# A new step order, one residual on TensorE and two more transposes by DMA in a two-block transformer kernel

## The chip, the cores and the metric

The kernel runs on one core of one Trainium2 chip. A core has five engines that run beside each other and meet through semaphores: TensorE (PE in the profile, with PEld for its weight loads), VectorE (DVE), ScalarE (ACT), GpSimd (POOL) and SyncE (SP, which here issues DMAs). The metric is the device time of one launch in microseconds (us). Before, three runs took 214.1, 212.67 and 212.69 us; their median is 212.69.

## The reference

The input x has 2048 rows of 512 elements in bf16. Two blocks follow each other, each with a layer norm ahead and a residual around it:

```
h  = x + A(layernorm(x))
h2 = h + B(layernorm(h))

A: qkv = x @ wqkv (512 x 1536), 32 heads of 16
   each position attends to 8 positions: itself and those 2, 4, ... 14 before it
   logits = q . k * 16**-0.5, those before the start masked; softmax over the 8; sum of v; @ wo (512 x 512)
B: gate = x @ W_gate, up = x @ W_up (512 x 1376)
   h = relu(gate) * up;  h @ W_down (1376 x 512)
layernorm: (x - mean) / sqrt(var + 1e-5), with no weights
```

## The kernel before

**Tiles.** The 2048 rows are four chunks (0 to 3, `tk` in the code) of 512 rows, each of four blocks of 128 rows. The whole of x stays in one tile `x_sm`, which the first residual overwrites in place with h. All weights are resident. Working tiles come from small pools that are shared by purpose: 9 `quad` tiles (a transposed norm, q, or the attention output: 128 x 4 x 512), 5 `big` tiles (128 x 8 x 512, the products of the attention), 5 `row` tiles (one normalised block of 128 x 512, or one output block), and 8 PSUM banks named `bank`, which every matmul group takes and an eviction frees.

**Stages of one chunk**, with the names that the steps carry below:

- first norm of x: statistics on VectorE (L420, L423), a logarithm and an exponential on ACT (L433, L437), the normalised blocks `xxn` on VectorE (L455, into `row`), and their transposes into a `quad` tile
- q, k and v: 12 groups of four 128x512 matmuls (L525, 4 x 0.216 us = 0.864 us), each evicted by ACT (L533)
- scores: products `pr` of q with eight shifted views of k on VectorE (L572, 2.2 us each, four a chunk), summed within heads on PE (L578), an exponential on ACT (L594), the denominators `den` on PE (L611), a logarithm and an exponential for their reciprocal on ACT (L614, L617). Chunk 0 scales with that reciprocal at the end (steps `om`, L667); chunks 1 to 3 scale the weights early (`am`, L626)
- weights spread back to channels on PE (L639, steps `bc`), evicted by ACT (L645); products `mu` with v on VectorE (L660, 2.2 us each, four a chunk); their sum over eight positions as a tree. In chunks 0 to 2 the first level of the tree is an accumulating DMA that GpSimd issues (L692, steps `ta`, 512 KB each); the rest is VectorE (L663, L686)
- `wo` on PE (L712, four groups of four matmuls, one group a block) and the first residual (L723): VectorE adds x and writes h into `x_sm`, with the row sums for the second norm
- second norm of h: mean and squares (L401 on VectorE, L409 on ACT with a sum), L430 and L437 on ACT, `hxn` on VectorE (L455), and transposes into a `quad` tile, hnT
- up and gate: 22 groups (L750, steps `mmu` and `mmg` by slice 0 to 10 of the 1376 columns), evicted by ACT (L754, and L757 with the relu), multiplied on VectorE (L770, steps `gu`, two slices at a time, each from a pair of tiles of which there are two)
- down: four blocks, each in two pieces of 8 and 3 matmuls (L787, steps `dn` a and b), the second residual on VectorE (L798, steps `o`), and the store by SP (L802, steps `os`). The last block of chunk 3 is cut in two halves of 256 columns.

**Two ways to transpose.** A normalised block is transposed either by four identity matmuls on PE (L484), with ACT evicting two blocks at once (L500; VectorE for two blocks of chunk 0, L498), or by a transposing DMA that SP issues from the `row` tile straight into the `quad` tile (L473). The tuple `DMAT` lists the pairs of blocks that go by DMA, each as (norm, chunk, first block): x of chunk 3 and h of chunks 2 and 3.

**Order.** The code first lists all steps (`add`), each with its engine and what it depends on. `RANK` holds one number per step, in the order of listing. Each engine runs its steps in the order of that number, so every queue (PE, VectorE, ACT, SP, GpSimd) is fixed by hand, and a step whose operands are late holds all that is behind it on its engine. `Plan.order` walks through the queues with assumed durations to choose which buffer of a pool each step takes. The chunks overlap widely: the products q, k, v of chunks 1 to 3 run on PE while VectorE works on chunk 0's attention, and the MLP of one chunk runs beside the attention of later ones.

**Around the change.** On VectorE, before: `xxn` of chunk 2, then mu3, mu0 of chunk 0, two `xxn` of chunk 3, mu1, mu2, and the other two `xxn` of chunk 3. SP issues each transpose as its block is ready. GpSimd issues `ta` as each `mu` is ready. The settings read by the changed code are `DMAT` (L468) and `RPE` (L406 to L411, L712 to L729), the chunks whose first residual goes to PE; before it is empty.

Of the kernel before, what the change touches and what calls it, by code (L numbers as in the profile page):

```python
# [15 lines left out]


RANK = [
    0, 1, 2, 3, 4, 5, 6, 7, 8, 9, 10, 11, 12, 13, 14, 15, 16, 18, 19, 21,
    25, 27, 28, 17, 20, 22, 24, 26, 31, 34, 38, 30, 35, 37, 39, 41, 44, 47, 23, 29,  # L20
    32, 33, 36, 40, 43, 50, 62, 71, 46, 64, 69, 42, 53, 65, 48, 52, 55, 56, 74, 67,
    77, 76, 82, 72, 79, 88, 90, 95, 148, 89, 97, 84, 99, 101, 94, 112, 118, 122, 78, 86,
    93, 96, 100, 157, 169, 192, 127, 134, 133, 138, 141, 102, 115, 110, 121, 105, 158, 167, 202, 206,
    211, 170, 182, 226, 231, 234, 180, 188, 229, 233, 236, 146, 159, 199, 204, 208, 244, 249, 241, 246,
    247, 253, 238, 243, 256, 262, 252, 254, 257, 260, 248, 250, 265, 269, 274, 277, 276, 280, 283, 278,
    282, 281, 285, 289, 313, 317, 321, 343, 335, 339, 345, 353, 358, 326, 337, 292, 300, 298, 336, 315,
    327, 347, 330, 351, 346, 355, 338, 359, 348, 356, 364, 319, 325, 296, 302, 309, 314, 301, 305, 331,
    357, 365, 341, 362, 352, 374, 366, 376, 383, 354, 371, 361, 368, 382, 417, 433, 459, 545, 380, 430,
    456, 460, 372, 389, 424, 461, 405, 414, 454, 463, 49, 59, 45, 57, 54, 60, 51, 58, 61, 63,
    73, 80, 68, 83, 85, 66, 81, 70, 87, 91, 163, 172, 152, 181, 104, 107, 142, 153, 106, 113,  # L30
    136, 176, 130, 145, 161, 174, 116, 155, 120, 164, 165, 178, 98, 103, 212, 193, 235, 239, 237, 219,
    251, 258, 263, 267, 273, 286, 284, 304, 312, 307, 311, 308, 290, 295, 293, 297, 299, 318, 324, 367,
    370, 334, 344, 375, 379, 342, 349, 386, 388, 322, 333, 373, 377, 395, 399, 400, 408, 392, 397, 398,
    403, 401, 404, 410, 413, 402, 406, 407, 409, 415, 416, 419, 423, 420, 425, 427, 422, 428, 421, 426,
    431, 438, 453, 445, 449, 437, 440, 443, 446, 464, 488, 502, 491, 496, 483, 500, 480, 490, 520, 470,
    477, 457, 469, 448, 455, 434, 458, 479, 465, 472, 475, 492, 452, 467, 478, 485, 494, 522, 537, 513,
    534, 462, 482, 517, 538, 546, 526, 540, 524, 528, 542, 543, 552, 556, 668, 530, 555, 566, 569, 539,
    553, 582, 586, 549, 557, 568, 587, 111, 124, 92, 108, 117, 123, 75, 109, 129, 131, 137, 156, 135,
    147, 160, 140, 150, 144, 149, 162, 186, 203, 184, 189, 201, 207, 179, 228, 194, 200, 183, 185, 205,
    217, 224, 230, 195, 198, 175, 223, 197, 209, 171, 220, 266, 259, 287, 291, 294, 288, 306, 316, 328,  # L40
    332, 340, 363, 360, 369, 378, 385, 381, 384, 387, 396, 393, 394, 391, 441, 450, 486, 489, 435, 444,
    481, 484, 429, 436, 466, 468, 412, 439, 471, 474, 498, 505, 495, 499, 509, 515, 501, 508, 514, 518,
    504, 506, 519, 521, 512, 523, 525, 527, 532, 550, 533, 536, 529, 541, 544, 547, 602, 607, 620, 626,
    597, 617, 593, 609, 630, 577, 581, 563, 583, 574, 592, 571, 576, 604, 588, 590, 594, 599, 584, 601,
    580, 605, 613, 567, 572, 565, 573, 561, 564, 559, 562, 579, 627, 641, 623, 632, 634, 639, 631, 645,
    649, 606, 616, 589, 648, 651, 646, 656, 658, 667, 652, 657, 683, 726, 636, 660, 663, 666, 655, 659,
    661, 664, 114, 126, 128, 143, 132, 139, 119, 125, 151, 154, 166, 177, 190, 196, 168, 173, 187, 191,
    227, 242, 210, 214, 264, 275, 215, 245, 218, 222, 255, 272, 261, 270, 221, 225, 232, 240, 213, 216,
    268, 329, 271, 279, 303, 310, 320, 323, 390, 350, 411, 418, 432, 442, 447, 503, 451, 507, 516, 531,
    511, 510, 473, 487, 497, 493, 476, 535, 558, 575, 595, 560, 570, 578, 598, 585, 591, 596, 603, 548,  # L50
    551, 554, 600, 608, 611, 610, 614, 612, 625, 615, 622, 619, 624, 618, 621, 628, 629, 633, 635, 637,
    638, 644, 654, 640, 643, 642, 653, 647, 650, 679, 692, 670, 688, 662, 695, 684, 687, 697, 691, 703,
    672, 675, 694, 699, 682, 685, 706, 689, 693, 698, 702, 686, 690, 677, 700, 705, 669, 676, 674, 678,
    671, 673, 665, 680, 681, 710, 715, 696, 712, 701, 717, 707, 709, 719, 708, 711, 704, 714, 716, 720,
    727, 729, 737, 723, 728, 731, 734, 713, 722, 724, 725, 718, 721, 733, 735, 730, 732, 736, 738,
]


# [129 lines left out]
def kernel(  # L188
# [147 lines left out]
    DAL = 5.5  # L336
    TDD, TDL = 1.25, 1.5
    NWARM, NFILL = 44, 8
    DMAT = (('h',2,0),('h',2,2),('x',3,0),('x',3,2),('h',3,0),('h',3,2))

    EARLY = (1, 2, 3)

    RPE, OPE = (), ()

    MERGE = (0, 1, 2, 3)

# [39 lines left out]
    def layernorm(tk, src, dst_slots, pr, groups, on_act, residual=None):  # L386
# [7 lines left out]
        for grp in groups:  # L394
# [72 lines left out]
            for j0 in range(lo, hi, step):  # L467
                if (ln, tk, j0) in DMAT:  # L468
                    for j in range(j0, min(j0 + step, hi)):
# [385 lines left out]
```

## Time and profile before

| | |
|---|---|
| three runs | 214.1, 212.67, 212.69 us (median 212.69) |
| the profiled execution: its time | 214.1 us |
| its span, first to last instruction | 212.3 us |
| mean granted TensorE clock | 0.984 |
| PE busy | 196.1 us |
| VectorE, ACT, GpSimd busy | 155.4, 121.9, 12.9 us |
| up and gate, 352 matmuls (L750) | 84.4 us |
| q, k, v, full-width groups of four (L525) | 0.864 us each at the full clock |
| transposes by DMA (L473) | 12 |
| accumulating DMAs (L692) | 12, median 6.0 us to landing |
| first residual (L723) | 16 x 0.684 us on VectorE |

The profile shows one execution. A row of a timeline has the start and the length in us, the engine, the line, the operation, the tiles (out<-in), shapes, and in brackets the idle time before it with what ended it. A busy PE is not proof of a PE at its peak, since matmuls are pipelined; the granted clock tells how fast it ran. The chain that ended last goes back from the last instruction, at each step to what released it. Busy times are sums over the whole span, and the limits differ from stage to stage.

### The profile page before, as it was taken

The numbers are of one execution on the slowest core, as the hardware profiler recorded it, in microseconds if no ns is written. First come the engines' busy times: TensorE is split into PE (matmuls) and PEld (weight loads), VectorE is DVE, ScalarE is ACT, GpSimd is POOL, SyncE is SP. The second block draws the span as 40 slices with busy tenths as digits, with TensorE's granted clock in tenths as the row PEclk, the third lists the DMA queues.
The fourth block names the chain that finished last, engine by engine and source line by source line (L and its number), as shares of the span: only waits on it lengthen the run. The fifth ranks groups of instructions, "written<-read, shape, count | busy, mean of one in ns | idle before, by whom it ended". The sixth has DMA issues, their size and how long they took to land.

```text
span 212.3 us, 2963 instructions
## 1 busy us (share of the span) xinstructions
PE 196.1 (92%) x1119; PEld 95.9 (45%) x1119; DVE 155.4 (73%) x247; ACT 121.9 (57%) x249; POOL 12.9 (6%) x29
## 2 busy tenths in 40 slices
PE   7699899980699999999999999999999999999993
PEld 7475345530243444444445444444444444444542
DVE  6678999997534999999999977599995642022213
ACT  3467699750176998659773759950445850167500
POOL 3000002300000000230002400000000000000000
PEclk9999999998599999999999999999999999999999
DMA  5689951998200000397000992032010022200012
GB/s 180 215 246 398 394 162 38 181 167 65 43 3 0 0 0 3 67 191 137 3 0 0 198 204 74 0 74 49 28 49 0 0 56 46 99 0 0 0 48 79
DMA packets 16589, 18.57 MB, mean 87 GB/s; under 512 B 7264, under 2 KB 13376, under 8 KB 16576
## 3 DMA queue, kind: packets, MB, share of 16 engines
q0 software_dynamic: 1728, 6.29, 18.2%
q1 hardware_dynamic: 14272, 11.31, 17.6%
q10 hardware_dynamic: 576, 0.79, 1.2%
q8 instruction: 9, 0.15, 0.3%
q14 instruction: 4, 0.03, 0.0%
HBM read 8.42 MB, written 2.10 MB: 50 GB/s over the span
## 4 chain that ended last, share of the span: by engine, by line
PE 61%; DVE 23%; DMA 12%; issue 2%; ACT 0%; POOL 0%; DVEq 0%; ACTq 0%; POOLq 0%
PE bank L750 27%; PE bank L787 18%; DVE big L572 10%; DVE big L660 7%; DMA x_sm<-in_A_x_dram 7%; PE bank L712 7%; PE bank L525 6%; DMA quad<-row 5%; DVE st L420 2%; DVE row L455 1%; PE bank L578 1%; DVE gT L770 1%; DVE ex L626 1%; PE bank L484 0%; PE bank L639 0%
## 5 line engine op out<-in xcount | busy, mean ns | idle before, releaser
L750 PE MATMUL bank<-quad,wg_sb 128*128 128x512 bf16 (+1 forms) x176 | 42.2, 379 | 0.1
L750 PE MATMUL bank<-quad,wu_sb 128*128 128x512 bf16 (+1 forms) x176 | 42.2, 379 | 0.0
L754 ACT CAST up_sb<-bank 128x512 bf16<-128x512 f32 (+1 forms) x44 | 24.8, 595 | 26.4 <-PE bank L750 18.8
L525 PE MATMUL bank<-quad,wqk_sb 128*128 128x512 bf16 (+1 forms) x144 | 30.9, 364 | 9.5 <-DMA quad<-row 8.3
L787 PE MATMUL bank<-wd_sb,gT 128*128 128x512 bf16 (+3 forms) x187 | 39.6, 367 | 0.1
L572 DVE TENSOR_TENSOR big<-quad,kT 128x4096 bf16<-128x4096 bf16 x16 | 36.0, 2282 | 1.0 <-ACT kT L533 1.0
L660 DVE TENSOR_TENSOR big<-big,vT 128x4096 bf16<-128x4096 bf16 x16 | 36.0, 2283 | 0.1
L757 ACT ACTIVATE gr<-bank 128x512 bf16<-128x512 f32 (+1 forms) x44 | 25.6, 607 | 15.4 <-PE bank L750 14.8
L770 DVE TENSOR_TENSOR gT<-gr,up_sb 128x1024 bf16<-128x1024 bf16 (+1 forms) x24 | 15.1, 640 | 18.4 <-ACT gr L757 12.4
L787 PEld LDWEIGHTS <-gT 128*128 128x128 bf16 (+1 forms) x187 | 18.1, 98 | 20.0 <-issue 0.7
L750 PEld LDWEIGHTS <-wu_sb 128*128 128x128 bf16 (+1 forms) x176 | 17.6, 100 | 20.6 <-issue 0.4
L750 PEld LDWEIGHTS <-wg_sb 128*128 128x128 bf16 (+1 forms) x176 | 17.5, 100 | 20.6 <-issue 0.9
L525 PEld LDWEIGHTS <-wqk_sb 128*128 128x128 bf16 x144 | 15.8, 115 | 22.3 <-issue 10.9
L663 DVE TENSOR_TENSOR big<-big 128x1024 bf16<-128x1024 bf16 (+2 forms) x24 | 16.9, 730 | 3.5 <-DMA big<-big 3.4
L723 DVE SCALAR_TENSOR_TENSOR x_sm<-x_sm,bank 128x512 bf16<-128x512 bf16 x16 | 10.8, 684 | 10.4 <-PE bank L712 10.1
L645 ACT CAST big<-bank 128x512 bf16<-128x512 f32 x32 | 17.2, 606 | 1.8 <-PE bank L639 1.8
L798 DVE TENSOR_TENSOR row<-x_sm,bank 128x512 bf16<-128x512 bf16 (+1 forms) x17 | 10.7, 651 | 10.3 <-PE bank L787 10.3
L692 POOL DMA_DIRECT2D big<-big x12 | 10.5, 901 | 99.1 <-DVE big L660 96.8
L533 ACT CAST kT<-bank 128x512 bf16<-128x512 f32 x16 | 9.3, 615 | 12.5 <-PE bank L525 12.5
L525 PE MATMUL bank<-quad,wv_sb 128*128 128x512 bf16 x64 | 16.2, 396 | 0.0
L712 PE MATMUL bank<-wo_sb,quad 128*128 128x512 bf16 x64 | 14.7, 379 | 0.0
L455 DVE TENSOR_SCALAR row<-x_sm,mv,rs 128x512 bf16<-128x512 bf16 x32 | 11.5, 403 | 4.2 <-ACT rs L437 4.2
(63 smaller groups left out, 143.0 us busy)
## 6 DMA issues: line engine op xcount, KB each, us to landing
big<-big POOLq DMA_DIRECT2D x12, 512.0 KB, 6.0
out_dram<-row SPq DMA_DIRECT2D x15, 128.0 KB, 1.8
x_sm<-in_A_x_dram SPq DMA_DIRECT2D x3, 512.0 KB, 6.3
wu_sb<-in_B_W_up_dram SPq DMA_DIRECT2D x1, 1376.0 KB, 9.7
wg_sb<-in_B_W_gate_dram SPq DMA_DIRECT2D x1, 1376.0 KB, 12.8
wd_sb<-in_B_W_down_dram SPq DMA_DIRECT2D x1, 1280.0 KB, 15.7
wqk_sb<-in_A_wqkv_dram ACTq DMA_DIRECT2D x2, 256.0 KB, 7.0
wqk_sb<-in_A_wqkv_dram SPq DMA_DIRECT2D x2, 256.0 KB, 7.2
```

What stands on the lines that cost most here:

```text
L455: V.tensor_scalar(out=xn.t[:], in0=x, scalar1=mv.t[:, j, 0:1], scalar2=rs.t[:, j:j + 1], op0=ALU.add if residual else ALU.subtract, op1=AL ...
L525: nc.tensor.matmul(mm.t[:, lo:hi], lhsT=wv_sb[:, dt, t:D:NT] if c == 2 else wqk_sb[:, dt, c * D + t:(c + 1) * D:NT], rhs=xnT.t[:, dt, lo:h ...
L572: V.tensor_tensor(out=pb.t[:].rearrange("p (t w) s -> p t w s", t=2), in0=q4, in1=k4, op=ALU.mult)
L645: nc.scalar.copy(out=ab.t[:, w, :], in_=bc.t[:])
L660: V.tensor_tensor(out=mt.t[:], in0=ab.t[:], in1=v8, op=ALU.mult)
L663: V.tensor_tensor(out=mt.t[:, 0:n, :], in0=mt.t[:, 0:n, :], in1=mt.t[:, n:2 * n, :], op=ALU.add)
L712: nc.tensor.matmul(od.t[:], lhsT=OT.t[:, t, j * P:(j + 1) * P], rhs=wo_sb[:, t, :], start=(t == 0), stop=(t == NT - 1 and tk not in RPE))
L750: nc.tensor.matmul(mm.t[:fs, :], lhsT=w_sb[:, dt, ft * P: ft * P + fs], rhs=hnT.t[:, dt, :], start=(dt == 0), stop=(dt == NT - 1))
L754: nc.scalar.copy(out=ub.t[:fs, i, :], in_=um.t[:fs, :])
L757: nc.scalar.activation(out=gr.t[:fs, i, :], in_=gm.t[:fs, :], func=ACT.Relu)
L770: V.tensor_tensor(out=gt.t[:fs, 0:n, :], in0=gr.t[:fs, 0:n, :], in1=ub.t[:fs, 0:n, :], op=ALU.mult)
L787: nc.tensor.matmul(od.t[:, c0:c1], lhsT=gts[ft].t[:fs, ft % 2, j * P:(j + 1) * P], rhs=wd_sb[:fs, ft, c0:c1], start=(ft == 0), stop=(ft == ...
```

## The change

Three settings differ; no other code does.

- `DMAT` gets ('h', 1, 0): blocks 0 and 1 of the second norm of chunk 1 are transposed by DMA (two steps `htd` on SP) in place of eight matmuls on PE and one eviction on ACT.
- `RPE` gets chunk 0: the first residual of chunk 0 is a fifth matmul in each of the four `wo` groups (identity times the block of `x_sm`, L715), ACT instead of VectorE writes h into `x_sm` with the row sums (L721), and the squares of the second norm of chunk 0 read h from the PSUM bank instead of from `x_sm` (L409).
- `RANK` is a new list: there are 738 steps instead of 739, and the order on every engine is another.

```
-    DMAT = (('h',2,0),('h',2,2),('x',3,0),('x',3,2),('h',3,0),('h',3,2))
+    DMAT = (('h',2,0),('h',2,2),('x',3,0),('x',3,2),('h',3,0),('h',3,2),('h',1,0))
...
-    RPE, OPE = (), ()
+    RPE, OPE = (0,), ()
```

The new RANK, sorted by engine, around the places that the prediction speaks of (the number after the point is the chunk; groups of products are named by q, k or v and their quarter):

```
VectorE before: ... xxn[1].2 xxn[0].2 xxn[2].2 xxn[3].2 mu3.0 mu0.0 xxn[0].3 xxn[2].3 mu1.0 mu2.0 xxn[3].3 xxn[1].3 pr0.1 ...
VectorE after:  ... xxn[0].2 xxn[1].2 xxn[2].2 xxn[3].2 xxn[1].3 xxn[3].3 xxn[0].3 xxn[2].3 mu3.0 mu0.0 mu1.0 mu2.0 pr0.1
                tree3.0 tree3.0 om3.0 pr0.1 tree0.0 tree1.0 tree0.0 tree1.0 om0.0 tree2.0 tree2.0 om1.0 om2.0 ...
SP after:       xtd[0].3 xtd[2].3 xtd[1].3 xtd[3].3 htd[0].1 htd[1].1 os0.0 os2.0 ...

PE before:      ... v3.2 v1.2 k1.2 k2.2 k0.2 q0.2 q2.2 v0.2 v2.2 q1.2 q3.2 | k0.3 v1.3 k1.3 q2.3 k3.3 k3.2 q0.3 v0.3 sc0.1 wo3.0 ...
PE after:       ... k3.2 k0.2 v0.2 q2.2 den.0 v3.2 q3.2 | q1.3 k1.2 q1.2 k2.2 q0.3 v3.3 q0.2 v1.3 k1.3 k0.3 q3.3 v0.3 v1.2
                wo0.0 wo1.0 wo3.0 wo2.0 sc0.1 sc1.1 q2.3 k2.3 den.1 k3.3 v2.2 hnT.0 transposes ...
                (the bar marks the first product of chunk 3)

PE before:      dn2a.0 dn1a.0 bc1.2 dn2b.0 wo2.1 wo0.1 wo3.1 wo1.1 dn3a.0 sc1.3 dn3b.0 dn0a.0 four transposes of hnT.1 ...
PE after:       dn2a.0 bc1.2 wo1.1 wo0.1 wo3.1 wo2.1 dn0a.0 sc1.3 dn3a.0 dn1a.0 dn0b.0 htp[3].1 dn1b.0 htp[2].1 dn3b.0
                den.3 dn2b.0 mmg2.1 ...

ACT after:      ... dl.0 v0.2 q1.2 dr.0 ... v0.3 rs0.0 v1.2 rs1.0 hsq[0].0 rs3.0 rs2.0 hsq[3].0 hsq[1].0 ex0.1 ex1.1 hsq[2].0
                hrl.0 hre.0 dl.1 ...   (dl and dr: the reciprocal, L614 and L617; rs: L721; hsq: L409)
PE after, end:  ... dn1a.3 mmu10.3 dn2a.3 dn0a.3 dn4a.3 dn0b.3 dn4b.3 dn2b.3 dn1b.3 dn3a.3 dn3b.3
                (before it ended with a half block, dn4a.3 dn4b.3)
```

## The prediction

> **What bounds the kernel now.** I read the page's busy shares first, then the chain that ended last in order of time, then TensorE's timeline, then short windows around its one long idle time.
>
> ```profile
> PE 196.1 (92%) x1119; PEld 95.9 (45%) x1119; DVE 155.4 (73%) x247; ACT 121.9 (57%) x249; POOL 12.9 (6%) x29
> 41.80 0.41 DVE row L455
> 42.20 1.81 DVE big L572
> 44.01 11.03 DMA quad<-row
> 55.04 0.14 issue
> 55.17 8.84 PE bank L525 x32
> ```
>
> PE is the bound. The chain runs through a DMA only once after the loads: from 44.01 to 55.04 it is a transpose of the first norm of chunk 3 (quad<-row), which PE waits for. TensorE's timeline, with start, length and idle time before it:
>
> ```profile
> 44.99 1.89 PE L525 MATMUL bank<-quad,wqk_sb 128*128 128x512 bf16 x8
> 55.17 1.87 PE L525 MATMUL bank<-quad,wqk_sb 128*128 128x512 bf16 x4 [8.29 <-DMA quad<-row]
> 56.84 1.91 PE L525 MATMUL bank<-quad,wv_sb 128*128 128x512 bf16 x4
> ```
>
> PE idles from 46.88 to 55.17, then takes 1.7 us for four matmuls that elsewhere take 0.86. The windows (third from the end: granted clock; then the DMA share) show why:
>
> ```profile
> 46.00:48.00 2.00, 0.88 (x5) 0.23 (x2) 2.00 (x4) 1.07 (x2) 0.00 (x0) 1.00 1.94 104
> 52.00:54.00 2.00, 0.00 (x0) 0.00 (x0) 0.00 (x0) 0.00 (x0) 0.00 (x0) 0.50 0.92 152
> 56.00:58.00 2.00, 2.00 (x6) 0.74 (x5) 1.02 (x4) 0.59 (x1) 0.00 (x0) 0.50 0.00 0
> ```
>
> The clock halves some 5 us into the idle time and stays so until about 58.5: eight matmuls at 0.427 instead of 0.216 us, 1.69 more. So the stall costs 8.29 + 1.69 = 9.98 us. From 55.17 to 208.80 PE has no idle time worth naming; VectorE in turn waited in the same stretch, 2.73 us for an accumulating DMA and 6.00 for PE:
>
> ```profile
> 54.69 1.36 DVE L663 TENSOR_TENSOR big<-big 128x1024 bf16<-128x1024 bf16 x3 [2.73 <-DMA big<-big]
> 66.00 0.69 DVE L723 SCALAR_TENSOR_TENSOR x_sm<-x_sm,bank 128x512 bf16<-128x512 bf16 x1 [6.00 <-PE bank L712]
> ```
>
> Why the transposes were late: asked one by one, the four were issued at 37.18, 38.6, 41.9 and 44.01 and landed 6.4, 6.4, 12.7 and 11.0 us later; the eight of chunks 2 and 3 near 139 and 171, with nothing beside them, took 2.4 to 2.5. Beside the slow ones ran chunk 0's four accumulating DMAs (L692), issued at 34.61, 36.82, 39.90 and 41.85, landing after 4.8, 6.2, 10.1 and 12.8.
>
> **The change, part by part.** Sorting the steps by the new RANK gives each engine's order; durations are the rows of before.
>
> *1. Transposes of x, chunk 3.* VectorE now does all four norms of chunk 3 before the first product mu3.0 (L660), not two after the second and two after the fourth. mu3.0 began at 32.07; a norm takes 0.33, so the norms end near 33.4 and mu3.0 at 35.6. The first block that SP issues is ready with the third norm; with the 0.4 us that SP took at 36.8, the issues (1.25 each unloaded) come at 33.4, 34.7, 35.9, 37.2. Below: the last lands 2.4 later, 39.6. Above: 12.7 later, 49.9. The first accumulate follows at 36.0 (before: 34.61), so the last block meets the first two accumulates, as before's first two blocks did at 6.4 us. I take that row: 43.6.
> PE comes to chunk 3 with five groups of four matmuls fewer behind it (six products of chunk 2 put off, one brought forward): 46.88 - 5 x 0.864 = 42.6. Gap: 43.6 - 42.6 = **1.0** (0 to 7.3). After 1.0 us of idle time the clock should hold, as it did over the 0.84 us gap at 9.8. Gain here 9.98 - 1.0 = 9.0.
>
> The Trainium skill (Advanced Engine Details and Errata, X-Bar Transpose) says that transposing DMAs are as fast as regular ones. This case differs: 11.0 to 12.7 us for 128 KB beside accumulates, against 1.8 for a 128 KB output. By the rule the gap would be 0 and the time 1.0 lower.
>
> *2. Chunk 0's first residual on PE.* Four identity matmuls on PE: 4 x 0.216 = **0.86** on the bound. VectorE loses four L723 with their read-outs (66.00 to 69.28, some 2.8 busy). ACT gets four reads of PSUM with a sum: not in the trace, between the plain eviction (0.48 from start to start) and the square with a sum (0.72 + 0.19); I take 0.8, as the nearest form. These now alternate with the squares, which read PSUM in place of x_sm (taken as unchanged, 0.1 either way). Queued behind them on ACT are chunk 1's two exponentials, and PE's den.1 waits for those. Forward: PE 43.6 + 13 groups = 54.8; the four wo.0 groups of 1.08 to 59.1; two score groups and two products to 62.8. ACT: rs0 from 56.1, then rs, squares and an eviction, ex1.1 ends near 63.2. So PE waits **0.6** for den.1. Then den, two products and the transposes of hnT.0 end near 66.9, against 75.55 before with one product more done (0.86). Lead 7.8: of the 9.0, about 1.1 is gone.
> VectorE must deliver OT.0 by 54.8. It ends mu2.0 at 42.2, pr0t2.1 at 44.4 and two tree steps at 45.3; then om3.0 waits for the reciprocal (L617), which ACT now holds behind an eviction of the third product after the gap: 43.6 + 2.6 + 0.7 + 0.6 = 47.5. With om3.0, a 2.2 product and 3.8 of tree steps: 53.9. Covered by 0.9 only.
>
> *3. Stage of the first MLP.* Behind the norms of h.0 (66.0) VectorE has two am (0.7), eight 2.2 us products up to mu2.1 (17.6), gu0, am0.2, gu1, another 2.2, gu3, four tree steps, gu2: 25.1, so 91.1 where before ended gu2.0 at 98.65. PE's 24.3 us of work there end beside it; with the banks that ACT frees last I put the first down projection at 92.0 instead of 99.47. Lead **7.5**.
>
> *4. Half of hnT.1 by DMA.* Off PE: eight transposes, 0.45 by the sixteen in 1.30; off ACT one L500 of 0.96; on SP two issues. wo.1 moves ahead of two down pieces; its operands are ready at 93.3, PE there at 94.1. The new wait is at the up and gate products of chunk 1: PE arrives at 92.0 + 15.81 - 0.45 = 107.4. The two norms end at 101.5 and 102.2 (wo.1's last sum 98.3, a product, two gate steps); SP issues at 101.9 and 103.2 and nothing is ahead of it. Queued behind them are only outputs. Unloaded: 105.6, no wait. Beside one accumulate (ta3.2, issued about 101.0): up to 6.4, 109.6. At 12.7: 115.9, a wait of 8.5. Only one accumulate is near, so I take the middle of the two lower rows and a wait of **0.5**.
>
> The page VectorE: DVE Perf Modes, section The three transpose paths, gives 390 ns for a 128x128 on TensorE and 1309 by DMA. That speaks against this part: eight tiles in a row, 10.5 us by the estimate, would land at 112.4, PE would wait 5.0 and the time be 211.1. The trace has 2.4 for a block of four tiles, which decides.
>
> *5. Tail and other order.* The last output piece is a whole one: 0.68 instead of 0.42, landing 1.9 instead of 1.6: **+0.4** to 0.6. For waits of the new order that I do not see I add **0.5**; between 99.5 and 208.8 before had none.
>
> **Sum.** 7.5 + 0.45 - 0.5 - 0.4 - 0.5 = 6.5 us less. The profiled execution took 214.1 (span 212.3); the other two 212.7. If its 1.4 more lay in the removed gap, the gain on the median is 5.1 (207.6); if elsewhere 6.5 (206.2). I say **206.6**.
>
> **Rivals.**
> - *Everything covered* (12%): chunk 3 lands by 42.6, no wait at den.1, hnT.1 or elsewhere: 1.0 + 0.6 + 0.5 + 0.5 more: 204.0, or 203.6 if the tail is free too. For it: the DMA share is 0.00 from 32 to 36. Against: the last issue falls behind ta3.0.
> - *The late block stays late* (17%): the fourth transpose takes 12.7, gap 7.3 and a cold restart of 1.69. Gain 9.98 - 8.99 = 1.0, less 0.86 for the residual and 0.4, plus 0.45: 212.5. For it: two of four did so. Against: those met four accumulates.
> - *ACT or VectorE takes over* (11%): the lead runs into VectorE, which has no idle time from 69.4 to 106, or into ACT's longer queue before den.1. VectorE had 9.7 us of waits before 66 to give up, but only 2.8 of work goes. At half the gain: 209.6; at none, with the tail: 213.1.
> - *Slower* (10%): hnT.1's blocks meet ta.2's accumulates as chunk 3's did ta.0's, land at 115.9, PE waits 8.5 and restarts cold: 8.5 + 1.69 - 0.5 = 9.7 more, 216.3. It turns slower once they land after about 112, with the cold restart. For it: the DMAs ahead and behind are of the same two kinds. Against: mu1.2's accumulate is issued only at 105.8.
> - *Nothing of it happens* needs no chance: both settings only select code that is there (L473 for two more blocks, L715 and L721 for chunk 0), and the order is read from RANK.
>
> **Chances.** The forecast, 205.0 to 208.5, has 50%. Range: 203.5 to 212.6, from the covered case to the late block; it leaves out part of the first and the slower case. Within 1% (210.6 to 214.8), about what a measurement can tell from no change: half of the late block and half of the takeover, 15%. With the rest of those two, the forecast and the covered case: faster 75%; slower 10%.
>
> **What would show it.** Right: no idle time over 2 us at the first product of chunk 3, near 43, and the clock at full speed there; four matmuls at L715; ACT with four sums at L721 between 56 and 61 and PE waiting under 1 us at L611; L750 of chunk 1 starting near 107 to 108. Wrong: PE waiting for quad<-row for over 4 us at either place, or idle time of PE at L639, L578 or L750 put down to ACT or DVE.

## The result, and the profile after

The changed kernel takes **203.38 us** in the median (202.19 to 204.01, six runs) against 212.69 (211.59 to 214.1, six runs) before. The ratio is 0.955 with a 95% interval of 0.9506 to 0.9595: faster by some 9.3 us. The prediction was 206.6 with a range from 203.5; the direction and the place of the gain were right, the size was short by 3.2 us, and the median lies 0.12 us under the range's lower end. The profiled execution took 203.08 us, its span is 201.3 us, the mean granted clock 1.0.

The page's busy shares of the changed kernel:

```profile
span 201.3 us, 2960 instructions
...
PE 194.4 (97%) x1115; PEld 96.0 (48%) x1115; DVE 153.1 (76%) x239; ACT 121.9 (61%) x256; POOL 12.8 (6%) x29
```

PE's busy time fell by only 1.7 us (196.1 to 194.4), about what the eight half-speed matmuls had cost. The rest is idle time that is gone: the span less PE's busy time was 16.2 us and is 6.9.

The chain of work that ended last, in order of time (start, length, what), from two stretches:

```profile
34.95 1.26 SPq L473
36.21 0.05 issue
36.27 4.94 DMA quad<-row
41.21 0.14 issue
41.34 11.39 PE bank L525 x52
...
100.83 3.51 DMA quad<-row
104.34 0.14 issue
104.47 3.61 PE bank L750 x16
```

The same kind of DMA that took 11.03 us in this chain before takes 4.94 now, and it starts at 36.27 instead of 44.01. The chain passes over one new DMA, the transpose of hnT.1 (3.51).

TensorE's timeline (start and length in us, then in brackets the idle time before the row), the rows that matter:

```profile
8.82 0.41 PE L525 MATMUL bank<-quad,wqk_sb 128*128 128x256 bf16 x2 [0.60 <-DMA wqk_sb<-in_A_wqkv_dram]
...
41.34 4.48 PE L525 MATMUL bank<-quad,wqk_sb 128*128 128x512 bf16 x20 [0.71 <-DMA quad<-row]
...
53.43 0.38 PE L715 MATMUL bank<-x_sm,identity 128*128 128x512 bf16 x1
...
60.57 0.59 PE L611 MATMUL bank<-ex,same 128*128 128x512 bf16 x2
...
88.55 1.89 PE L787 MATMUL bank<-wd_sb,gT 128*128 128x512 bf16 x8
...
104.47 1.02 PE L750 MATMUL bank<-quad,wg_sb 128*128 128x512 bf16 x4 [0.40 <-DMA quad<-row]
```

The 8.29 us of idle time at chunk 3 are 0.71 now, and twenty matmuls follow in 4.48 us, which is full speed. The two rows with brackets at 41.34 and 104.47 are PE's only waits of 0.2 us or more after the first 10 us. The first down projection begins at 88.55 instead of 99.47, and this lead of 10.9 us is kept to the end.

The transposes at L473, and GpSimd's issues of the four accumulating DMAs:

```profile
L473 SPq DMA_TRANSPOSE quad<-row x14: 1196/1238/2176, 32.3 to 164.0; - x14
...
DMA to landing us min/median/max: 2.4/2.5/4.9
```

```profile
35.44 1.01 POOL L692 DMA_DIRECT2D big<-big  x1 [25.24 <-PE bank L525]
...
42.01 0.86 POOL L692 DMA_DIRECT2D big<-big  x1 [1.34 <-DVE big L660]
```

Chunk 3's four are issued at 32.3, 33.7, 35.0 and 36.3 and land after 2.5, 2.5, 2.8 and 4.9 us. The first accumulate is issued at 35.44: the third block barely meets it, and only the last one is slowed.

### The profile page after: what moved, and what is told of

It reads as the page before. It is cut to its first block, busy times and chain, and to the rows that moved or that the text cites. A ratio compares the mean times of both kernels' runs of the same rounds, so it can differ in the third digit from the quotient of the medians.

```text
span 201.3 us, 2960 instructions
## 1 busy us (share of the span) xinstructions
PE 194.4 (97%) x1115; PEld 96.0 (48%) x1115; DVE 153.1 (76%) x239; ACT 121.9 (61%) x256; POOL 12.8 (6%) x29
## 4 chain that ended last, share of the span: by engine, by line
PE 55%; DVE 24%; DMA 11%; ACT 5%; issue 2%; SPq 1%; POOL 0%; DVEq 0%; ACTq 0%; POOLq 0%
PE bank L750 29%; PE bank L787 14%; DVE big L572 7%; DMA x_sm<-in_A_x_dram 7%; DVE big L660 7%; PE bank L525 6%; PE bank L712 5%; DMA quad<-row 4%; DVE st L420 2%; DVE row L455 2%; DVE gT L770 2%; DVE x_sm L723 1%; DVE big L663 1%; ACT big L645 1%; ACT row L409 1%
## 5 line engine op out<-in xcount | busy, mean ns | idle before, releaser
L750 PE MATMUL bank<-quad,wg_sb 128*128 128x512 bf16 (+1 forms) x176 | 42.5, 379 | 0.4 <-DMA quad<-row 0.4
L750 PE MATMUL bank<-quad,wu_sb 128*128 128x512 bf16 (+1 forms) x176 | 42.7, 379 | 0.1
L572 DVE TENSOR_TENSOR big<-quad,kT 128x4096 bf16<-128x4096 bf16 x16 | 36.2, 2283 | 0.1
L750 PEld LDWEIGHTS <-wg_sb 128*128 128x128 bf16 (+1 forms) x176 | 17.3, 100 | 21.3 <-issue 0.9
L750 PEld LDWEIGHTS <-wu_sb 128*128 128x128 bf16 (+1 forms) x176 | 17.5, 100 | 20.6 <-issue 0.7
L645 ACT CAST big<-bank 128x512 bf16<-128x512 f32 x32 | 17.8, 638 | 0.4 <-PE bank L639 0.4
L525 PE MATMUL bank<-quad,wv_sb 128*128 128x512 bf16 x64 | 15.7, 380 | 0.0
L712 PE MATMUL bank<-wo_sb,quad 128*128 128x512 bf16 x64 | 15.3, 379 | 0.0
L533 ACT CAST quad<-bank 128x512 bf16<-128x512 f32 x16 | 9.4, 609 | 4.5 <-PE bank L525 4.5
L500 ACT COPY quad<-bank 128x1024 bf16<-128x1024 bf16 (+1 forms) x9 | 8.0, 930 | 6.3 <-PE bank L484 6.2
## 6 DMA issues: line engine op xcount, KB each, us to landing
wg_sb<-in_B_W_gate_dram SPq DMA_DIRECT2D x1, 1376.0 KB, 12.7
```

What stands on the lines that cost most here:

```text
L525: nc.tensor.matmul(mm.t[:, lo:hi], lhsT=wv_sb[:, dt, t:D:NT] if c == 2 else wqk_sb[:, dt, c * D + t:(c + 1) * D:NT], rhs=xnT.t[:, dt, lo:h ...
L572: V.tensor_tensor(out=pb.t[:].rearrange("p (t w) s -> p t w s", t=2), in0=q4, in1=k4, op=ALU.mult)
L645: nc.scalar.copy(out=ab.t[:, w, :], in_=bc.t[:])
L712: nc.tensor.matmul(od.t[:], lhsT=OT.t[:, t, j * P:(j + 1) * P], rhs=wo_sb[:, t, :], start=(t == 0), stop=(t == NT - 1 and tk not in RPE))
L750: nc.tensor.matmul(mm.t[:fs, :], lhsT=w_sb[:, dt, ft * P: ft * P + fs], rhs=hnT.t[:, dt, :], start=(dt == 0), stop=(dt == NT - 1))
```

## The experiments

Each ratio is to runs of the kernel before on the same chip, with its 95% interval. The theory: the time is won by issuing chunk 3's transposes ahead of the accumulating DMAs, everything else is small. Rivals: the new order as a whole, the residual on PE, the half of hnT.1 by DMA, or the clock alone.

### Only the four norms earlier

The order of before; only the four first norms of chunk 3, with their statistics and ACT's two small steps for them, go ahead of mu3.0. Residual and hnT.1 stay as before.

```
+MOVED = {397: 132.04, 399: 132.03, 402: 132.05, 404: 132.06, 565: 132.02, 567: 132.01,
+         570: 133.01, 571: 134.01, 572: 132.07, 574: 132.1, 576: 132.08, 578: 132.09}
+RANK = [MOVED.get(n, r) for n, r in enumerate(RANK)]
```

> The kernel before, with only this moved: the four norms of chunk 3's x (and their statistics and exponential) stand ahead of mu3.0 on VectorE, as in the changed kernel; no residual on PE, no new transposes, the rest of the order as before. Theory (the early transposes are the whole gain): the four issues fall at 33 to 38, the last lands by 42, PE comes to chunk 3 only at 46.9 and finds no gap and no cold clock; 9.5 us less, 203.2 (202.5 to 206). Rival (the gain needs the other order on PE, the residual or the half by DMA): at least 209, with PE waiting for VectorE or ACT instead. Second rival (transposes beside accumulates are slow wherever they start): gap over 4 us, above 207.

Measured: 204.03 us against 213.23, ratio 0.9546 (0.9495 to 0.9597). The transposes of this kernel at L473:

```profile
L473 SPq DMA_TRANSPOSE quad<-row x12: 1195/1237/1297, 32.7 to 164.6; - x12
...
who waited for it (us, times):
busy tenths in 40 slices 0000000000000000000000000000000000000000
DMA to landing us min/median/max: 2.4/2.5/5.2
```

Chunk 3's four are issued at 32.7 to 36.7, land after 2.5, 2.5, 2.5 and 5.2 us, and the list of those who waited for them is empty: PE, in the old order, comes to chunk 3 later than they land. So moving twelve steps out of 739 gives the whole gain, within what the runs can tell.

### The changed kernel with the norms late again

```
+MOVED = {571: 168.01, 573: 187.01, 575: 168.02, 577: 187.02}
+RANK = [MOVED.get(n, r) for n, r in enumerate(RANK)]
```

On the changed kernel's RANK: two of chunk 3's norms go behind mu0.0 and two behind mu2.0, as before.

> The changed kernel with only this undone: two norms of chunk 3's x after mu0.0 and two after mu2.0 on VectorE, as before. Theory: the last transpose is issued near 43 and lands near 54; PE, which comes to chunk 3 at 40.6, waits 13 us and restarts at half clock; 12 to 14 us more, about 216. Rival (the order elsewhere carries the gain): under 206.

Measured: 216.06 against 213.23, ratio 1.0129 (1.0086 to 1.0172): 1.3% above the kernel before. TensorE's timeline, and one window of 2 us (third from the end: the granted clock):

```profile
51.63 6.85 PE L525 MATMUL bank<-quad,wqk_sb 128*128 128x512 bf16 x20 [10.44 <-DMA quad<-row]
```

```profile
52.00:54.00 2.00, 2.00 (x6) 0.73 (x5) 0.00 (x0) 0.00 (x0) 0.00 (x0) 0.50 0.00 0
```

The stall is back, longer than before since the new order brings PE to chunk 3 sooner, and the restart is cold: 6.85 us for the twenty matmuls that the changed kernel does in 4.48. Stall (10.44 - 0.71) and cold clock (2.37) make 12.1 of the some 12.7 us between this kernel and the changed one's 203.4. The late issue does most of it: the four are issued at 37.4, 39.0, 42.4 and 44.3 and land after 5.0, 6.3, 7.5 and 7.2 us, less than in the kernel before. The rest of the change, without the early norms, is a loss.

### No accumulating DMAs in chunk 0

On the kernel before, the first level of chunk 0's tree is done by VectorE:

```
-    ... for k in range(3) for t in range(4))
+    ... for k in (1, 2) for t in range(4))
```

> The kernel before, with the first tree level of chunk 0 on VectorE (four adds of 1.15 us) instead of four accumulating DMAs; everything computed. Theory (the transposes of chunk 3 are slow because the accumulates run beside them): each lands 2.4 to 2.6 us after its issue, the last near 46, PE's gap at chunk 3 is under 1 us, its clock stays full; VectorE's 4.6 us more cost 0 to 4; 203 to 207. Rival (slow for another reason, such as their late start alone or VectorE's products): landing 6 to 12 us as before, gap over 4, 213 to 217.

Measured: 207.53 against 213.23, ratio 0.9704 (0.9657 to 0.9752). TensorE's timeline and the transposes at L473:

```profile
48.72 1.03 PE L525 MATMUL bank<-quad,wqk_sb 128*128 128x512 bf16 x4 [2.45 <-DMA quad<-row]
```

```profile
DMA to landing us min/median/max: 2.4/2.5/2.5
```

With the accumulates gone, all four transposes land after 2.4 to 2.5 us, at the old place between VectorE's products. So it is the accumulates that make them slow. The idle time that is left, 2.45 instead of under 1 us as expected, comes from VectorE: its own additions now stand between the norms, so the last block is issued at 46.2 instead of 44.0. With this wait and two waits for VectorE behind it (0.46 and 0.63) PE accounts for most of the 3.5 us by which the time lies above the kernel with early norms.

### The kernel before, run again

No edit.

> The kernel before once more, to see how much its own stall and start vary: theory, the gap at chunk 3 is between 5 and 9 us and moves with the time of the run, and the q and k weights land between 6 and 7.2 us after their issue, so the start varies by about 1 us. Rival: the gap is 8.3 within 0.3 and the weights land at 7.0 to 7.2 always, so that the changed kernel's earlier start is due to the change.

Measured: 211.19 us. Its stall, in TensorE's timeline:

```profile
52.11 1.87 PE L525 MATMUL bank<-quad,wqk_sb 128*128 128x512 bf16 x4 [6.73 <-DMA quad<-row]
```

The stall is 6.73 us here and 8.29 in the execution that the prediction used; the landings are 6.4, 6.6, 11.0 and 9.4 us. The start differs too: the q and k weights land 5.5 to 6.5 us after their issue instead of 6.6 to 7.6, and the first accumulate is issued at 33.11 instead of 34.61. So the 211.2 to 214.4 us that the kernel before shows on this chip hold a moving stall and a moving start, about 1.5 us each between these two executions, and the prediction's profile had the larger stall of the two.

### The changed kernel without the residual on PE

```
-    RPE, OPE = (0,), ()
+    RPE, OPE = (), ()
```

VectorE does chunk 0's first residual again, in the new order.

> The changed kernel with the first residual of chunk 0 back on VectorE (its four steps at the places of the new order). Theory (the part is a shift of work with a small gain): PE loses 0.86 of work, VectorE gains 2.8 where it has only 0.9 us of waits, so the second norm of chunk 0 is 2 us later, PE waits about 2 us at its transposes and the first MLP starts 1 to 2 us later: 1.2 more than the changed kernel, 204.6 (203.4 to 205.5). Rival (as the prediction counted it, 0.86 on the bound and a wait at den.1): 0.9 to 1.5 less than the changed kernel, 202.

Measured: 205.67 against 213.67, ratio 0.9601 (0.9557 to 0.9645), 2.1 us above two kernels on the same chip that differ from the changed one by edits without effect (203.44 and 203.6, in the runs without the half of hnT.1 by DMA and with SP's other order below); 1.2 was expected. TensorE's timeline:

```profile
61.41 0.86 PE L611 MATMUL bank<-ex,same 128*128 128x512 bf16 x2 [0.54 <-ACT ex L594]
...
64.83 1.36 PE L484 MATMUL bank<-identity,row 128*128 128x128 bf16 x16 [0.84 <-DVE row L455]
```

In the new order VectorE's four additions stand among its 2.28 us products, so chunk 0's second norm is late and PE waits for it. The four matmuls cost PE 0.86 us and buy more than that, in this order.

### Early norms and the residual on PE, in the old order

The kernel with early norms plus `RPE = (0,)`, run beside the changed kernel and beside early norms alone, all on one chip (before: 213.95).

> The kernel before with the early norms of chunk 3 and the first residual of chunk 0 on PE, nothing else. With the early norms alone PE has no idle time of 0.3 us or more after the first 10 us. Theory (PE's work is now the floor): four more matmuls cost 0.86 although VectorE is freed of 2.8: 0.5 to 1.2 more than the early norms alone. Rival (VectorE still sets the first MLP): 0.5 to 1.5 less.

> The changed kernel again, beside the next two on one chip. Its first profile had the q and k weights 0.7 to 1.0 us earlier than most others; theory: with a later start its time is 203.4 to 204.2, ratio 0.950 to 0.957. Rival: the earlier start belongs to it, 202.5 to 203.4.

> The kernel before with the early norms of chunk 3 alone, again. Theory (this one move is the whole gain of the change, the residual, the half by DMA and the rest of the order cancel): the same as the changed kernel within 0.5. Rival: 1 us or more slower than the changed kernel.

Measured: both together 205.31, ratio 0.9614 (0.9575 to 0.9654); the changed kernel 203.56, 0.9537 (0.9494 to 0.9581); early norms alone 204.14, 0.9557 (0.9518 to 0.9596). In the old order the residual on PE costs 1.2 us: with early norms alone PE's longest idle time between 25 us and the end is 0.25 us, so an earlier second norm has nothing to fill, and the 0.86 us of work come on top. The changed kernel and the twelve moved steps can't be told apart by these runs.

### The changed kernel without the half of hnT.1 by DMA

```
-    DMAT = (('h',2,0),('h',2,2),('x',3,0),('x',3,2),('h',3,0),('h',3,2),('h',1,0))
+    DMAT = (('h',2,0),('h',2,2),('x',3,0),('x',3,2),('h',3,0),('h',3,2))
+RANK[312:315] = [425.01, RANK[313], 425.02, 430.99]
```

> The changed kernel with blocks 0 and 1 of the second norm of chunk 1 transposed by PE and evicted by ACT again. Theory (the half by DMA buys 0.45 us of PE and gives 0.4 back as a wait): the wait of 0.40 for the DMA at the first gate product of chunk 1 goes, eight transposes of 0.45 come: the same within 0.3, 203.4. Rival 1 (it frees ACT or PE): 0.5 to 1 more. Rival 2 (its wait is a real loss): 0.4 or more less.

Measured: 203.44 against 213.67, ratio 0.9509 (0.9467 to 0.9551): no difference from the changed kernel. The wait of 0.40 us at chunk 1's gate is gone, the 0.45 us of PE work are back.

### SP issues the blocks as the norms come

```
+MOVED = {574: 159.98, 578: 159.99}
+RANK = [MOVED.get(n, r) for n, r in enumerate(RANK)]
```

On the changed kernel's RANK: SP takes blocks 1, 3, 0, 2 of chunk 3 in place of 0, 2, 1, 3.

> The changed kernel with SP issuing the four transposes of chunk 3 in the order in which VectorE finishes the norms (1, 3, 0, 2 instead of 0, 2, 1, 3). Theory: the first issue is 0.6 us earlier, so the last one starts ahead of the first accumulate's data, lands 0.7 to 2 us earlier, and PE's wait of 0.71 at chunk 3 goes: 0.7 less, 202.7. Rival (the last block's norm sets the last issue, or the wait only moves to den.1 or VectorE): no difference.

Measured: 203.6 against 213.67, ratio 0.9513 (0.947 to 0.9556): no difference; the 0.7 us that were expected did not come. PE still waits 0.74 us at chunk 3: SP needs some 1.3 us for each issue, so the last block leaves at 36.8 and meets the accumulates in either order (landing after 5.6).

### Only the clock kept up

On the kernel before, 30 matmuls of no use ahead of chunk 3's first product:

```
-            def f_mm(lo=0, hi=CS, c=c, t=t, mm=mm, xnT=xnT):
+            def f_mm(lo=0, hi=CS, c=c, t=t, mm=mm, xnT=xnT, tk=tk):
+                for _ in range(30 if (tk, c, t) == (3, 1, 0) else 0):
+                    nc.tensor.matmul(mm.t[:], lhsT=wqk_sb[:, 0, 0:P], rhs=wv_sb[:, 0, :], start=True, stop=True)
                 for dt in range(NT):
```

> The kernel before, with 30 matmuls of other data (128x512, 6.5 us, their sum is overwritten) ahead of the first product of chunk 3, so that PE is busy through most of its wait for the transposes. Theory (the restart at half clock costs 1.69): idle time at chunk 3 under 2.5 us, granted clock full through 50 to 60, 1.7 less: 211.5 against 213.2 (ratio 0.992). Rival (VectorE or ACT limits the stretch behind the wait, so the cold restart is hidden): no difference.

Measured: 212.36 against 213.67, ratio 0.9913 (0.9878 to 0.9947): 1.3 us less in the medians, 1.9 by the ratio. The mean granted clock, 0.976 to 0.984 in the kernel before, is 0.998 to 1.0 in eleven of twelve executions and 0.992 in the one that was profiled. That fits the 1.69 us that the prediction gave to the cold restart. The rest of the stall stays: the last two transposes land after 12.8 and 11.1 us here too.

### VectorE idle beside the slow transposes

In the kernel before, the DMA rate falls to 18 to 63 GB/s from 47 to 51, and in that stretch VectorE runs two products (L572, 46.87 to 51.36). Here chunk 0's last tree steps, which wait for accumulates, go ahead of these products:

```
+MOVED = {103: 211.01, 104: 211.03, 105: 211.05, 108: 211.02, 109: 211.04, 110: 211.06}
+RANK = [MOVED.get(n, r) for n, r in enumerate(RANK)]
```

> The kernel before, with chunk 0's tree steps that wait for the third and fourth accumulating DMA (and the two om steps after them) put ahead of VectorE's next two products of chunk 1 (L572). VectorE then waits for the accumulates where before it ran those two products from 46.87 to 51.36, the stretch in which the DMA rate was 18 to 63 GB/s. If VectorE's products are what slows the DMAs, the rate stays near 150 to 200 GB/s from 46 on, the transposes of chunk 3 land within 8 us each, PE starts chunk 3 3 to 4 us sooner (near 51 to 52) and is idle 4 to 5 us there instead of 6.7 to 8.3. If the slow stretch comes from the transposes and accumulates alone, the landings stay at 9 to 13 us and the idle time at 6.5 to 8.5. The time says less: the products put off by some 5 us may cost PE up to that much later on, so 208 to 214 in the first case, 212 to 218 in the second.

Measured: 212.97 against 213.47, ratio 0.998 (0.9932 to 1.0028). TensorE's timeline, and two windows of 1 us (busy time of PE, PEld, VectorE, ACT and GpSimd, then the clock, the DMA share and GB/s):

```profile
54.57 1.87 PE L525 MATMUL bank<-quad,wqk_sb 128*128 128x512 bf16 x4 [8.59 <-DMA quad<-row]
```

```profile
47.00:48.00 1.00, 0.00 (x0) 0.00 (x0) 0.00 (x0) 0.00 (x0) 0.00 (x0) 1.00 1.28 43
48.00:49.00 1.00, 0.00 (x0) 0.00 (x0) 0.00 (x0) 0.00 (x0) 0.00 (x0) 1.00 1.55 37
```

No engine works in these two microseconds, and the rate is 43 and 37 GB/s all the same. So VectorE's products beside the slow stretch were a coincidence. It comes with the transposes and accumulates themselves, though not always when they meet (last section).

## Why the prediction was right, and where it was short

The mechanism was right; sizes of single terms failed, nearly all to the same side. In step 1 the last block landed after 4.9 us and not 6.4, and PE came to chunk 3 at 40.6 and not 42.6; in step 2 ACT's read with a sum took 0.58 us and not 0.8, and the wait of 0.6 us at den.1 did not occur; in step 5 the +0.4 of the tail and the 0.5 for unseen waits were nothing.

**What bounds the kernel: right.** The stall at chunk 3 and its cold restart were the whole prize. Early norms alone bring 9.2 us on medians and 9.8 in the repeat, beside the prediction's 9.98 from an execution with a longer stall than the other one (8.29 against 6.73).

**1. Transposes of x, chunk 3: right in kind, the largest miss in size.** Issue times are within 1.1 us of those predicted, the gap is 0.71 against 1.0, and the clock held. But PE restarts at 41.34, not 43.6: 2.3 us. Two terms failed, and they hid each other in the gap. The landing row: the last block, taken at 6.4 us, needs 4.9 here, and 5.0 to 5.7 in the seven other profiles with early norms, and it is issued at 36.3, not 37.2. It met less than the row it was taken from: when it lands, some 180 of the accumulates' 576 packets have started (144 make one accumulate); when before's first block landed, it was some 310. And PE's arrival, taken at 42.6, is 40.63 (41.34 - 0.71): the last wait for the weights ends at 8.82 instead of 9.78, and two small waits of before, 0.65 at 21.59 and 0.41 at 24.47, don't occur. Together 0.96 + 0.65 + 0.41 = 2.0. The weight wait moves between executions (9.08 in the repeat, where PE restarts at 41.92). The 0.65 goes with the order: none of the six profiles with the new order has this wait for L572, and seven of the eight with the old order have it at 0.2 to 0.7; early norms alone lack it once. The second wait moves too (0.37 in the repeat).

The rule of the Trainium skill that transposing DMAs are as fast as regular ones (Advanced Engine Details and Errata, X-Bar Transpose) gave a gap of 0. The gap is 0.60 to 0.87 in the five profiles with this order, so the rule stays wrong in this place, by less than the row of before made of it.

**2. Residual on PE: right with one term mis-sized.** The step "I take 0.8" for ACT's read with a sum was too dear. ACT's timeline after (start, length):

```profile
54.95 0.61 ACT L721 ACTIVATE x_sm<-bank 128x512 bf16<-128x512 f32 x1
55.44 0.21 ACT L721 ACTIVATION_READ_ACCUMULATOR x_sm<-bank 128x1 f32 x1
55.53 0.70 ACT L409 ACTIVATE row<-bank,mv 128x512 bf16<-128x512 f32 x1
```

From 54.95 to 55.53 it takes 0.58. The prediction's upper bound, 0.72 + 0.19 for a square with its sum, added two rows that overlap: in the kernel before, two squares in a row start at 70.07 and 70.78, 0.71 apart, and the middle between that and 0.48 is 0.6. With four of these ACT was some 0.9 us sooner, and the 0.6 us wait at den.1 did not occur: L611 at 60.57 has no idle time before it. From the restart of chunk 3 to the first up or gate product PE took 24.58 us, where the prediction's steps make 25.5. That this part pays only in the new order, the prediction did not say.

**3. Stage of the first MLP: right.** From the first L750 to the first down projection 22.63 us, 0.3 under the 22.9 of the prediction. The lead there is 10.9 instead of 7.5: 2.3 from step 1, 0.9 from step 2, 0.3 from this one.

**4. Half of hnT.1 by DMA: right.** The two blocks landed after 4.8 and 3.5 us and PE waited 0.40, against 0.5 predicted; taking the part out changes nothing that can be measured. The estimate from the Trainium skill's page VectorE: DVE Perf Modes (The three transpose paths) had a wait of 5.0 there; the rows of 2.4 to 6.4 us that the trace has for blocks of four tiles were the better guide.

**5. Tail and other order: wrong.** The step "+0.4" rests on a misreading. The last two parts of chunk 3 are both halves of 256 columns, in either order, so the tail is unchanged. The 0.5 for unseen waits met nothing.

**The sum.** Between the two profiled executions the gain is 214.1 - 203.08 = 11.0, where the steps gave 6.5. The difference is the 3.4 us of lead (steps 1 to 3), 0.4 for the tail, 0.5 for unseen waits and 0.1 at the gate. On medians 1.4 of it is the profiled execution of before having been the slowest of its runs, which the prediction shaded for by 0.4, and 0.3 is the profiled execution of after having been below its median. So the miss on medians is 4.5 - 1.4 - 0.3 + 0.4 = 3.2. Nearly every allowance had been made to the same side. Of the rivals "everything covered" (204.0, or 203.6 with a free tail) came nearest, though not by its own account: the gap stayed at 0.7 and PE arrived sooner instead. "The late block stays late" failed on its place in the queue: the block met little more than one accumulate, not four. "ACT or VectorE takes over" and the slower case found nothing in the trace.

## What to carry to other kernels

When PE waits for a DMA, ask which other DMAs are in flight beside it before making it smaller or moving it to another engine: here twelve steps moved in the engines' order gave 9.2 and 9.8 us, as much as the whole change within what the runs can tell, and the half by DMA gave nothing. Once the one long stall is gone PE is busy without a break, and then an added matmul is paid in full (0.86 us of work cost 1.2 here) unless another engine's delay is taken away with it. An estimate from one execution should be put against the spread of that stall, and its allowances should not all lean one way.

## What the runs showed of the hardware that was not expected

**Transposing DMAs and accumulating DMAs hold each other up, at times far beyond their sizes.** A block of 128 KB takes 2.4 to 2.5 us alone, 4.9 to 5.7 beside the first accumulates, and among all four 6.4 to 12.8 in the order of before, 5.0 to 7.5 in the changed kernel with late norms. The queues in the same 26 us (30 to 56) of two kernels, before and then after (packets, MB, share of 16 engines):

```profile
q0 software_dynamic: 576, 2.10, 63.1%
q1 hardware_dynamic: 2176, 0.52, 14.8%
```

```profile
q0 software_dynamic: 576, 2.10, 43.6%
q1 hardware_dynamic: 2176, 0.52, 10.0%
```

The same packets took some 45% more of the DMA engines' time in the kernel before. Most packets took no longer: the median 4 KB packet of an accumulate took 0.34 us in both. The excess lies in 25 of the 576 packets, which started between 46.29 and 48.90 and took 1.95 to 4.64 us each. The same stretch, from 46.2 to 49 us, in the kernel before and then in the changed kernel with late norms (a packet's whole time counts where it starts, so a share can exceed 100%):

```profile
q0 software_dynamic: 49, 0.18, 205.9%
```

```profile
q0 software_dynamic: 106, 0.39, 83.0%
```

That is 1.9 us a packet against 0.35. The repeat of before, the kernel with fillers and the one with VectorE idle each have 25 to 27 packets of 1.5 us or more as well. No profile with early norms has one, and neither has the changed kernel with late norms, where transposes and accumulates mix as much: its longest such packet took 1.1 us.

The Trainium skill (DMA: Bandwidth & Descriptors, Queues, rings and completion order) says that each DMA engine takes turns between the queues it has work for, packet by packet. Blocks that need 4.9 to 7.5 us beside accumulates, against 2.5 alone, fit that. It does not say why a packet of 4 KB should take 4.64 us, nor why the rate falls to 18 to 63 GB/s. That stays open: VectorE's products are ruled out (212.97 us, 8.59 us of stall), and the changed kernel with late norms keeps 162 to 196 GB/s from 44 to 50.

**The clock after some 2 us of idle time.** In the profiled execution of the kernel with fillers, the longest of its twelve, PE was idle for 1.96 us up to 54.06, and the clock was 0.75 in the window from 54 to 56 and 0.50 from 56 to 58; in that of the kernel without accumulates it stayed at 1.00 through an idle time of 2.45 us. Other executions of both went the other way: 0.998 to 1.0 on the mean with fillers, 0.992 to 0.996 in the three others without accumulates. The Trainium skill (TensorE: Matmul & The Clock Gate, What's actually happening) puts the fall after an idle window of about 3.4 us; the 1.96 us of the one execution fall short of that. What decides between the two was not tried.
